# A fused layer norm, FNet and MLP kernel: the first row block multiplied before it is scaled

## The chip, the cores and the metric

The kernel runs on one core of a Trainium2 chip. A core has TensorE (PE, the matmuls; PEld is its weight load, which runs beside them), VectorE (DVE), ScalarE (ACT), GpSimd (POOL) and SyncE (SP), each with an instruction queue of its own that is worked off strictly in order. The engines wait for one another through semaphores. Data moves between DRAM and SBUF by DMA; here SP issues most of the transfers, in order. The metric is the device time of one execution in microseconds (us), median of several runs.

## The reference

The input x has 2048 rows of 640 columns. Each row is normalized, and three terms are added: x itself, a two-dimensional Fourier transform of the normalized rows (real part, as products with DFT matrices), and an MLP.

```python
def _layernorm(x, axis=-1, eps=1e-5):
    m = jnp.mean(x, axis=axis, keepdims=True)
    v = jnp.var(x, axis=axis, keepdims=True)
    return (x - m) / jnp.sqrt(v + eps)

def _A_ref(x, dft_seq_re, dft_seq_im, dft_hid_re, dft_hid_im):
    a = jnp.einsum("bsd,ed->bse", x, dft_hid_re)
    b = jnp.einsum("bsd,ed->bse", x, dft_hid_im)
    return jnp.einsum("ts,bse->bte", dft_seq_re, a) - jnp.einsum("ts,bse->bte", dft_seq_im, b)

def _B_ref(x, w1, b1, w2, b2):
    h = jnp.einsum("bsd,df->bsf", x, w1) + b1
    h = _gelu(h)
    return jnp.einsum("bsf,fd->bsd", h, w2) + b2

xn = _layernorm(x, axis=-1)
return x + _A_ref(xn, ...) + _B_ref(xn, B_w1, B_b1, B_w2, B_b2)
```

All inputs are fp32; w1 is 640 x 1536, w2 is 1536 x 640.

## The kernel before, in words

*Tiling.* The 2048 rows are four row blocks of 512; 640 columns are five chunks of 128; the 1536 hidden units are twelve groups of 128, called units here. Activations stand in SBUF transposed, columns of x on the partitions and 512 rows along the free axis, since PE contracts over partitions.

*Precision.* Every operand of a product is split in two fp32r halves: the high half is a copy made by ACT (L160), the low half is the source minus the high half, made by DVE (L161). A product is then three matmuls of 128x512: high by high, high by low, low by high (`product`, L277 to L279). One unit of the first layer for one row block, `hidden(g)` (L301), is 5 chunks times 3 = 15 matmuls into one PSUM bank (bank g % 3); one unit of the second layer, `output(g)`, is again 15 matmuls, into the five banks 3 to 7, which collect all twelve units of a row block.

*Order.* The kernel is under a manual schedule: the order of the instructions on each engine is the order in which the code issues them. No planner moves anything; semaphores alone decide when an instruction starts.

*The start.* SP loads the first four row tiles x0 to x3 (128 rows each, `load_x`, L178) and then the weights: w1 by units (`load_w1`, L255, four transfers for a unit, into three rotating buffers called w1r), w2 by units (`load_w2`). Meanwhile PE works through 19 matmuls of zeros (NWARM, L648). Their three operand tiles lie in the w1r buffers, cast from `zeros` by DVE (L639); so a load of w1 into such a buffer waits until the warm matmuls that read it are done, and NGATE says after which of them that is (the 7th, the 10th, the last). The rows are normalized one way or another: x0 by DVE statistics (`ln_stats`, L185 and L186) and a scaling on ACT, x1 by sums on ACT (L672, L676 and four one-column steps), x2 and x3 by DVE statistics and `ln_apply_chunked` (L208). `ln_scale` makes 1/sqrt(var + eps) of a variance: a square root on ACT (L192) and five small DVE steps that refine it. The normalized rows go into the tile xp, PE transposes them by chunks into banks 3 to 7 (`transpose_x`, L667), ACT and DVE split these into XTT (tile xtt, five chunks of two halves), and `hidden(0)` starts.

*The loop.* The kernel's first two row blocks make 24 steps g (twelve units each). While `output(g)` runs, `hidden(g + 2)` is already computed, and ACT's gelu (L314) turns its bank into AB, a copy (L318) makes the high half hs, a DVE subtraction (L320) the low half. The order of one step of the first row block is

```python
prep_w1(i + 3)
prep_w2(i + 1)
load_w1(i + 6)
load_w2(i + 4)
first_block(i)
acc = hidden(g + 2)
gelu(g + 2, acc)
output(g)
```

and what `first_block(i)` issues stands on DVE, ACT and SP between those:

- i = 0 and 1: the rows of the first block are scaled on DVE once more, in natural order (`ln_apply`, L201), and stored to the DRAM scratch xs (L203), from which the transposed z comes back later; the next x tiles are loaded. i = 2 to 5: statistics of x4 to x7.
- i = 6: square root, scaling and stores of these rows; the load of z for the second row block; loads of x8 to x11.
- i = 8 and 9: DVE transposes z in blocks of 32 (`transpose_z`, L238) and makes statistics of x8 to x11. In step 9, between `hidden(11)` and `gelu(11)`, the five chunks of the second block's activations are split into XTT (`prep_xt`), each behind a transpose of z.
- i = 10: `load_xo(0)`, square root, scaling and stores of x8 to x11, loads of x12 to x15.
- i = 11: the first raw columns of the hidden DFT matrices are loaded (`load_w`, tile wraw, L364), and the finished banks of the first row block are added up (`add_block`: bias on ACT L344, DVE transpose L347, add on POOL L349).

In the second row block's steps the same hands prepare the later stages: DVE turns the DFT columns (`turn_w`, L372), ACT and DVE split them into wst, POOL's queue stores them to the scratch wit (`put_w`, L394), more z is transposed and more sums are formed. Behind step 23 stand `head` and `mid`, in which ACT copies whole banks (L810, L817) so that products can go on from a copy. From 182 us on PE works through the MLP of the other row blocks and the products of the Fourier transform.

## Time and profile before

| | |
|---|---|
| median of 3 runs (lowest to highest) | 853.95 us (853.48 to 853.95) |
| profiled execution: time, span | 853.7 us, 851.9 us |
| granted TensorE clock, mean over the span | 0.998 |
| instructions | 10326 |
| busy: PE, PEld, DVE, ACT, POOL | 842.7, 695.8, 661.1, 353.6, 48.1 us |
| PE busy from 0 to 13 us | 9.74 us |
| PE busy from 13 to 182 us | 169.00 us |
| PE busy from 182 us to the end | 663.93 of 670 us |

A row of the profile's list of groups names the line of the code, the engine, the operation, the tiles written and read, the shape, how often it ran, its busy time in all and the mean of one in ns, and how long the engine idled just before them, with what ended most of that idling. A row of the timeline begins with the start in us from the start of the span and the time that the row covers (several instructions of a kind are drawn together, with their count behind the x), and ends, in square brackets, with the idle time ahead of it and the instruction that ended it. In a list of waits the three numbers are the idle time in us, how often, and the longest.

A matmul's record is longer (0.39 us) than its turn on PE (0.227 us), since successive ones overlap; the turn is what counts for the length of a stream.

### The profile page before, as it was taken

The numbers are of one execution on the slowest core, as the hardware profiler recorded it, in microseconds if no ns is written. First come the engines' busy times: TensorE is split into PE (matmuls) and PEld (weight loads), VectorE is DVE, ScalarE is ACT, GpSimd is POOL, SyncE is SP. The second block draws the span as 40 slices with busy tenths as digits, with TensorE's granted clock in tenths as the row PEclk, the third lists the DMA queues.
The fourth block names the chain that finished last, engine by engine and source line by source line (L and its number), as shares of the span: only waits on it lengthen the run. The fifth ranks groups of instructions, "written<-read, shape, count | busy, mean of one in ns | idle before, by whom it ended". The sixth has DMA issues, their size and how long they took to land.

```text
span 851.9 us, 10326 instructions
## 1 busy us (share of the span) xinstructions
PE 842.7 (99%) x3711; PEld 695.8 (82%) x3711; DVE 661.1 (78%) x836; ACT 353.6 (42%) x496; POOL 48.1 (6%) x69
## 2 busy tenths in 40 slices
PE   8999999999999999999999999999999999999997
PEld 6888888878888888888888888888888888888885
DVE  7554766785758888879979787889967998885686
ACT  7443634456666554343444343232323423222241
POOL 0000211031211300000000000000000000000001
PEclk9999999999999999999999999999999999999999
DMA  7757698937669998958744679663865779704464
GB/s 186 215 143 199 142 228 233 225 81 190 206 223 349 360 208 161 185 110 200 160 137 105 168 215 293 159 145 97 208 169 169 252 191 228 303 19 179 125 179 99
DMA packets 207235, 158.45 MB, mean 186 GB/s; under 512 B 80848, under 2 KB 180688, under 8 KB 206672
## 3 DMA queue, kind: packets, MB, share of 16 engines
q1 hardware_dynamic: 198880, 136.03, 62.6%
q0 software_dynamic: 4080, 20.97, 6.2%
q10 hardware_dynamic: 4224, 0.79, 0.4%
q8 instruction: 29, 0.48, 0.2%
q14 instruction: 22, 0.18, 0.1%
HBM read 114.76 MB, written 42.99 MB: 185 GB/s over the span
## 4 chain that ended last, share of the span: by engine, by line
PE 98%; DVE 1%; DMA 0%; ACT 0%; issue 0%; SPq 0%; ACTq 0%
PE banks L277 29%; PE banks L279 29%; PE banks L278 29%; PE banks L301 10%; DMA x<-in_A_x_dram 0%; PE banks L667 0%; DVE st L185 0%; ACT ab L672 0%; DVE yo L1695 0%; ACT mv L192 0%; DVE mv L186 0%; DVE xp L208 0%; SPq L178 0%; DVE mv L194 0%; DVE mv L196 0%
## 5 line engine op out<-in xcount | busy, mean ns | idle before, releaser
L277 PE MATMUL banks<-as,xab 128*128 128x512 f32 x411 | 159.9, 389 | 0.0
L279 PE MATMUL banks<-as,xab 128*128 128x512 f32 x411 | 159.9, 389 | 0.0
L278 PE MATMUL banks<-as,xab 128*128 128x512 f32 x411 | 159.9, 389 | 0.0
L160 ACT ACTIVATE as<-r 128x1024 fp32r<-128x1024 f32 x80 | 85.0, 1062 | 177.0 <-PE banks L279 149.2
L161 DVE TENSOR_TENSOR as<-r,as 128x1024 fp32r<-128x1024 f32 x80 | 97.2, 1216 | 41.7 <-ACT as L160 41.6
L278 PEld LDWEIGHTS banks<-as,xab 128*128 128x128 f32 x411 | 77.1, 188 | 16.1
L277 PEld LDWEIGHTS banks<-as,xab 128*128 128x128 f32 x411 | 77.1, 188 | 16.1
L279 PEld LDWEIGHTS banks<-as,xab 128*128 128x128 f32 x411 | 77.1, 188 | 16.0
L277 PE MATMUL banks<-as,xc 128*128 128x512 f32 x224 | 87.1, 389 | 0.0
L278 PE MATMUL banks<-as,xc 128*128 128x512 f32 x224 | 87.1, 389 | 0.0
L279 PE MATMUL banks<-as,xc 128*128 128x512 f32 x224 | 87.1, 389 | 0.0
L160 ACT ACTIVATE as<-rt 128x1024 fp32r<-128x1024 f32 x32 | 34.0, 1063 | 70.8 <-PE banks L279 62.8
L301 PE MATMUL banks<-xtt,xab 128*128 128x512 f32 x240 | 56.9, 390 | 0.0
L301 PEld LDWEIGHTS banks<-xtt,xab 128*128 128x128 f32 x240 | 45.0, 188 | 9.7 <-ACT xtt L160 0.5
L278 PEld LDWEIGHTS banks<-as,xc 128*128 128x128 f32 x224 | 42.0, 188 | 8.8
L279 PEld LDWEIGHTS banks<-as,xc 128*128 128x128 f32 x224 | 42.0, 188 | 8.8
L277 PEld LDWEIGHTS banks<-as,xc 128*128 128x128 f32 x224 | 42.0, 188 | 8.7
L161 DVE TENSOR_TENSOR as<-rt,as 128x1024 fp32r<-128x1024 f32 x32 | 38.8, 1212 | 5.3 <-ACT as L160 5.3
L320 DVE TENSOR_TENSOR hs<-ab,hs 128x512 fp32r<-128x512 f32 x24 | 17.6, 733 | 32.2 <-ACT hs L318 32.2
L160 ACT ACTIVATE as<-u 128x1024 fp32r<-128x1024 f32 (+1 forms) x24 | 22.1, 919 | 48.2 <-PE banks L279 48.2
L488 DVE STREAM_TRANSPOSE r<-raw 128x1024 f32<-128x1024 f32 x32 | 39.5, 1240 | 2.3 <-PE banks L279 1.8
L488 DVE STREAM_TRANSPOSE rt<-raw 128x1024 f32<-128x1024 f32 x32 | 38.8, 1230 | 0.9 <-PE banks L279 0.8
(336 smaller groups left out, 1618.2 us busy)
## 6 DMA issues: line engine op xcount, KB each, us to landing
raw<-in_A_dft_seq_re_dram SPq DMA_DIRECT2D x64, 256.0 KB, 5.8
raw<-in_A_dft_seq_im_dram SPq DMA_DIRECT2D x64, 256.0 KB, 5.1
ws<-wit SPq DMA_DIRECT2D x15, 384.0 KB, 4.1
x<-in_A_x_dram SPq DMA_DIRECT2D x16, 320.0 KB, 4.1
xs<-x SPq DMA_DIRECT2D x64, 80.0 KB, 1.8
xo<-in_A_x_dram SPq DMA_DIRECT2D x16, 320.0 KB, 6.4
xab<-wit SPq DMA_DIRECT2D x13, 384.0 KB, 4.3
wit<-wstp POOLq DMA_DIRECT2D x12, 384.0 KB, 3.9
```

The source lines that it names most:

```text
L160: nc.scalar.activation(h, s, AF.Copy)
L161: nc.vector.tensor_tensor(l, s, h.bitcast(F32), op=ALU.subtract)
L277: nc.tensor.matmul(acc, wh, mh, start=first, stop=False, skip_group_check=goes_on)
L278: nc.tensor.matmul(acc, wh, ml, start=False, stop=False, skip_group_check=goes_on)
L279: nc.tensor.matmul(acc, wl, mh, start=False, stop=last, skip_group_check=goes_on)
L301: nc.tensor.matmul(acc, W1[i][:, a, j * P : (j + 1) * P], XT[j][:, b], start=n == 0, stop=n == len(steps) - 1)
L320: nc.vector.tensor_tensor(hs[:, 1], a, hs[:, 0].bitcast(F32), op=ALU.subtract)
L488: nc.vector.transpose(held(pieces[g][2], u).rearrange("p c (n i) -> p c n i", i=B), r.rearrange("p n (c i) -> p c n i", i=B))
```

## The change

In the first row block the rows are only centred before the transposes. The products of the first layer are made from the centred rows, and each row's 1/sqrt(var + eps) is multiplied onto the result of each of the block's twelve units, on DVE, ahead of the gelu. The factor is a number per row, and rows lie along the free axis there, so it has to stand on all 128 partitions: ACT writes each factor 128 times side by side (`wide`), four PE transposes inside `hidden(2)` (`spread`, after its first ASIDE = 4 matmuls) turn that into bank 7, and DVE copies it to the tile RB, which takes one of the two places with the tag yt.

With it go these edits. x0 and x2 get their means from the DVE statistics and x1 and x3 from sums on ACT; the variances of x1 and x3 are made later, by ACT's squares of the centred rows behind `hidden(1)`'s operands, and one square root for all four tiles follows there; a gelu of one column comes ahead of the spreading copy. The warm matmuls are 12 instead of 19, with one operand tile that lies in the place "as" and no longer in w1's buffers, so that w1's first three loads wait for none of them; the load of w1's first unit is cut in two (chunks 0 and 1, then 2 to 4), and its halves are split in two parts as well. w1's third unit is split between the squares and the square root, ahead of the split of w2's first unit instead of behind it. `output(0)` runs its 15 matmuls in another order: for all five banks those with the high half of hs first, then those with the low half.

```diff
--- before.py
+++ after.py
@@ -17,9 +17,9 @@
 Q = 4
 B = 32
 EPS = 1e-5
-NWARM = 19
-NGATE = (7, 10)
+NWARM = 12
 TAIL = 4
+ASIDE = 4
 PADL = 8
 
 
@@ -245,14 +245,15 @@
 
     W1, W2, w1r, w2r = {}, {}, {}, {}
 
-    def load_w1(i, eng=nc.sync):
+    def load_w1(i, eng=nc.sync, cuts=(0, ND)):
         if i >= NF:
             return
         t = early.tile([P, ND, P], F32, tag="w1r", bufs=3, name=f"w1r{i}")
         w1r[i] = t
...
-        for q in range(Q):
-            eng.dma_start(t[q * B : (q + 1) * B], v[q, :, :, i * P : (i + 1) * P])
+        for c0, c1 in zip(cuts, cuts[1:]):
+            for q in range(Q):
+                eng.dma_start(t[q * B : (q + 1) * B, c0:c1], v[q, :, c0:c1, i * P : (i + 1) * P])
 
     def load_w2(i, eng=nc.sync):
         if i >= NF:
@@ -286,7 +287,7 @@
     def unit(g):
         return g if g < NF else LATE[g % NF]
 
-    def hidden(g):
+    def hidden(g, aside=None):
         i = unit(g)
         acc = bank(g % 3)
         kinds = ((0, 0), (0, 1), (1, 0))
@@ -297,6 +298,8 @@
 
             steps.sort(key=lambda s: s[1] == 2)
         for n, (j, k) in enumerate(steps):
+            if aside and n == ASIDE:
+                aside()
             a, b = kinds[k]
             nc.tensor.matmul(
                 acc, W1[i][:, a, j * P : (j + 1) * P], XT[j][:, b], start=n == 0, stop=n == len(steps) - 1
@@ -311,6 +314,9 @@
 
         i = unit(g)
         a = AB[:, g % 2]
+        if g < NF:
+            nc.vector.tensor_tensor(a, acc, RB, op=ALU.mult)
+            acc = a
         nc.scalar.activation(a, acc, AF.Gelu_apprx_tanh, bias=b1c[:, i : i + 1])
         fill(0)
         hs = HS[:, g % 3]
@@ -319,11 +325,27 @@
         fill(1)
         nc.vector.tensor_tensor(hs[:, 1], a, hs[:, 0].bitcast(F32), op=ALU.subtract)
 
+    def first_output(hs):
+        w = W2[0]
+        for k in range(2):
+            for e in range(ND):
+                cols = slice(e * P, (e + 1) * P)
+                if k == 0:
+                    nc.tensor.matmul(oacc[0][e], w[:, 0, cols], hs[:, 0], start=True, stop=False)
+                    nc.tensor.matmul(oacc[0][e], w[:, 1, cols], hs[:, 0], start=False, stop=False)
+                else:
+                    nc.tensor.matmul(
+                        oacc[0][e], w[:, 0, cols], hs[:, 1], start=False, stop=False, skip_group_check=True
+                    )
+
     def output(g):
         t, i = divmod(g, NF)
         if i == 0:
             oacc[t] = [bank(3 + e) for e in range(ND)]
-        second(t, i, unit(g), HT[g])
+        if g == 0:
+            first_output(HT[g])
+        else:
+            second(t, i, unit(g), HT[g])
 
     def second(t, i, u, hs, es=range(ND)):
         for e in es:
@@ -628,23 +650,26 @@
 
     zeros = rows.tile([P, TB], F32, tag="yt", bufs=2, name="zeros")
 
-    warms = [early.tile([P, TB], F32R, tag="w1r", bufs=3, name=f"warm{k}") for k in range(3)]
+    RB = rows.tile([P, TB], F32, tag="yt", bufs=2, name="rb")
 
     for c in range(NC):
         load_x(c)
+    for tag, size, keys in PLACES:
+        t = whole[tag] = place(tag, (P, size // 4))
+        for k, key in enumerate(keys):
+            slots[key] = t[:, k * 2 * D : (k + 1) * 2 * D].rearrange("p (a b) -> p a b", a=2)
     nc.gpsimd.memset(eps, EPS)
     make_identity(nc, ident)
     nc.vector.memset(zeros, 0.0)
-    for warm in warms:
-        nc.vector.tensor_copy(warm, zeros)
+    warm = whole["as"][:, :TB]
+    nc.vector.tensor_copy(warm, zeros)
 
     nc.scalar.activation(eps[:, 1:2], eps[:, 0:1], AF.Sqrt)
-    load_w1(0)
+    load_w1(0, cuts=(0, 2, ND))
     load_w1(1)
 
     wacc = bank(0)
     for k in range(NWARM):
-        warm = warms[sum(k >= n for n in NGATE)]
         nc.tensor.matmul(wacc, warm[:, :P], warm, start=True, stop=True)
     load_w1(2)
     load_w2(0)
@@ -652,10 +677,6 @@
     load_w2(1)
     load_w2(2)
 
...
     for j in range(ND):
         new_xt(0, j)
     tacc = [bank(3 + j) for j in range(ND)]
@@ -667,50 +688,55 @@
             nc.tensor.transpose(tacc[j][:, c * P : (c + 1) * P], xp[:, c, j * P : (j + 1) * P], ident)
 
 
-    m = MV[:, 1]
-    scratch = AB.rearrange("p a b -> p (a b)")
-    nc.scalar.activation(scratch[:, :D], xt[1], AF.Copy, accum_out=m[:, 4:5])
-    ln_stats(0)
-    ln_scale(0, 1)
-    nc.scalar.activation(m[:, 5:6], m[:, 4:5], AF.Copy, scale=-1.0 / D)
-    nc.scalar.activation(scratch[:, :D], xt[1], AF.Square, bias=m[:, 5:6], accum_out=m[:, 2:3])
-    nc.scalar.activation(m[:, 1:2], m[:, 2:3], AF.Copy, scale=1.0 / D)
-    nc.scalar.activation(m[:, 0:1], m[:, 5:6], AF.Copy, scale=-1.0)
-
-    def center(c):
-        n = MV[:, c]
-        nc.vector.scalar_tensor_tensor(n[:, 5:6], n[:, 0:1], -1.0, n[:, 3:4], op0=ALU.mult, op1=ALU.mult)
-
-    def apply_on_act(c, j0, j1):
-        n = MV[:, c]
-        nc.scalar.activation(
+    scratch = AB.rearrange("p a b -> p (a b)")[:, :D]
+
+    def sum_on_act(c):
+        nc.scalar.activation(scratch, xt[c], AF.Copy, scale=-1.0 / D, accum_out=MV[:, c, 5:6])
+
+    def square_on_act(c):
+        nc.scalar.activation(scratch, xp[:, c], AF.Square, scale=D**-0.5, accum_out=MV[:, c, 1:2])
+
+    def center(c, op, shift, j0=0, j1=ND):
+        nc.vector.tensor_scalar(
             chunked(xp[:, c])[:, :, j0:j1],
             xt[c].rearrange("p (q c i) -> p q c i", q=Q, i=B)[:, :, j0:j1],
-            AF.Identity,
-            bias=n[:, 5:6],
-            scale=n[:, 3:4],
+            shift,
+            None,
+            op0=op,
         )
 
-    center(0)
-    apply_on_act(0, 0, ND)
-    for c in (2, 3):
-        ln_stats(c)
+    W1[0], first_w1 = slots[1, 0], w1r.pop(0).rearrange("p a b -> p (a b)")
+
+    def first_hi(j0, j1):
+        nc.scalar.activation(W1[0][:, 0, j0 * P : j1 * P], first_w1[:, j0 * P : j1 * P], AF.Copy)
+
+    def first_lo(j0, j1):
+        h, l = (W1[0][:, k, j0 * P : j1 * P] for k in range(2))
+        nc.vector.tensor_tensor(l, first_w1[:, j0 * P : j1 * P], h.bitcast(F32), op=ALU.subtract)
+
+    sum_on_act(1)
+    nc.scalar.activation(
+        chunked(xp[:, 1]), xt[1].rearrange("p (q c i) -> p q c i", q=Q, i=B), AF.Identity, bias=MV[:, 1, 5:6]
+    )
+    ln_stats(0)
+    center(0, ALU.subtract, MV[:, 0, 0:1])
+    ln_stats(2)
+    center(2, ALU.subtract, MV[:, 2, 0:1])
+    sum_on_act(3)
+    center(3, ALU.add, MV[:, 3, 5:6], 0, 2)
+    center(3, ALU.add, MV[:, 3, 5:6], 2, ND)
+    first_hi(0, 2)
+    first_lo(0, 2)
     transpose_x(0, 0, ND)
-    ln_scale(1, 3)
-    center(1)
-
-    W1[0], first_w1 = slots[1, 0], w1r.pop(0).rearrange("p a b -> p (a b)")
+    transpose_x(1, 0, ND)
     for j0, j1 in ((0, 2), (2, ND)):
-        apply_on_act(1, j0, j1)
-        if j0 == 0:
-            nc.scalar.activation(W1[0][:, 0], first_w1, AF.Copy)
-        for c in (2, 3, 1):
-            if c != 1:
-                ln_apply_chunked(xp[:, c], c, j0, j1)
-            transpose_x(c, j0, j1)
-    nc.vector.tensor_tensor(W1[0][:, 1], first_w1, W1[0][:, 0].bitcast(F32), op=ALU.subtract)
+        transpose_x(2, j0, j1)
+        transpose_x(3, j0, j1)
     for j in range(ND):
         split(XT[j][:, 0], XT[j][:, 1], tacc[j])
+        if j == 1:
+            first_hi(2, ND)
+            first_lo(2, ND)
     load_w1(3)
     load_w1(4)
     for q in range(Q):
@@ -718,8 +744,28 @@
     acc0 = hidden(0)
     prep_w1(1)
     acc1 = hidden(1)
+
+    nc.gpsimd.tensor_scalar(MV[:, 1::2, 0], MV[:, 1::2, 5], -1.0, None, op0=ALU.mult)
+    square_on_act(1)
+    square_on_act(3)
+    W1[2] = slots[1, 2]
+    raw2 = w1r.pop(2).rearrange("p a b -> p (a b)")
+    nc.scalar.activation(W1[2][:, 0], raw2, AF.Copy)
+    ln_scale(0, NC)
+    nc.scalar.activation(eps[:, 1:2], eps[:, 0:1], AF.Gelu_apprx_tanh)
+    nc.vector.tensor_tensor(W1[2][:, 1], raw2, W1[2][:, 0].bitcast(F32), op=ALU.subtract)
+    wide = AB[:, 1]
+    nc.scalar.activation(
+        wide.rearrange("p (c n) -> p c n", c=NC), MV[:, :, 3:4].broadcast_to([P, NC, P]), AF.Copy
+    )
+
+    def spread():
+        for c in range(NC):
+            nc.tensor.transpose(bank(7)[:, c * P : (c + 1) * P], wide[:, c * P : (c + 1) * P], ident)
+
+    acc2 = hidden(2, spread)
     prep_w2(0)
-    prep_w1(2)
+    nc.vector.tensor_copy(RB, bank(7))
     load_w2(3)
     load_w1(5)
 
@@ -1023,7 +1069,7 @@
                 output(g)
                 gelu(g + 2, hidden(g + 2))
             else:
-                acc = hidden(g + 2)
+                acc = hidden(g + 2) if g else acc2
                 if i == NF - 3:
                     for j in range(ND):
                         prep_xt(1, j)
```

More of the change, by code (lines that the diff above doesn't have):

```diff
@@ L653 @@
     load_w2(2)
-    for tag, size, keys in PLACES:
-        t = whole[tag] = place(tag, (P, size // 4))
-        for k, key in enumerate(keys):
-            slots[key] = t[:, k * 2 * D : (k + 1) * 2 * D].rearrange("p (a b) -> p a b", a=2)
     for j in range(ND):
```

## The prediction

> **What bounds the kernel now.** I read the page first (engines, chain), then what PE waited for, then the first 30 us and the stretch from 57 to 182 us as a timeline.
>
> ```profile
> span 851.9 us, 10326 instructions
> ...
> PE 842.7 (99%) x3711; PEld 695.8 (82%) x3711; DVE 661.1 (78%) x836; ACT 353.6 (42%) x496; POOL 48.1 (6%) x69
> ...
> PE 98%; DVE 1%; DMA 0%; ACT 0%; issue 0%; SPq 0%; ACTq 0%
> ```
>
> PE is busy 99% of the span and carries 98% of the chain, so the time is the moment at which PE's stream begins plus every gap in it. Only two lists of waits matter: PE's own at the start, and its weight loads' (PEld), which show where ACT or DVE already arrive at the last moment.
>
> ```profile
> PE banks L667 <- DVE xp L208: 1.3, 1, 1.3
> ```
>
> ```profile
> PEld banks L277 <- ACT banks L810: 0.5, 2, 0.3
> ```
>
> The first is the layer norm ahead of the transposes. The second lies at 182 us: there ACT has no room at all, and whatever is late on ACT or DVE by then is paid by PE. The median of the runs is 853.95; the profiled execution took 853.7 (851.9 and 1.8 around the span), 0.25 less, and I add the change to the median.
>
> **Part 1: the start.** Rows of the first 30 us, and two groups and a landing view of the same stretch:
>
> ```profile
> 3.77 0.89 DVE L185 BATCH_NORM_STATS2 st<-x 128x6 f32<-128x320 f32 x2 [1.23 <-DMA x<-in_A_x_dram]
> ...
> 9.85 1.51 DVE L208 TENSOR_SCALAR xp<-x,mv 128x256 f32<-128x256 f32 x4
> ...
> 21.12 0.69 DVE L320 TENSOR_TENSOR hs<-ab,hs 128x512 fp32r<-128x512 f32 x1 [1.63 <-ACT hs L318]
> 21.75 0.82 DVE L161 TENSOR_TENSOR xab<-w1r,xab 128x640 fp32r<-128x640 f32 x1
> ```
>
> ```profile
> 4.51 0.74 ACT L672 ACTIVATE ab<-x 128x640 f32<-128x640 f32 x1 [2.28 <-DMA x<-in_A_x_dram]
> ...
> 5.65 0.83 ACT L676 ACTIVATE ab<-x,mv 128x640 f32<-128x640 f32 x1
> ...
> 11.70 2.52 ACT L160 ACTIVATE xtt<-banks 128x512 fp32r<-128x512 f32 x5
> ...
> 16.12 1.28 ACT L314 ACT_TABLE_LOAD   x1
> 17.41 0.69 ACT L314 ACTIVATE ab<-banks,b1c 128x512 f32<-128x512 f32 x1
> 18.13 0.63 ACT L318 ACTIVATE hs<-ab 128x512 fp32r<-128x512 f32 x1
> ```
>
> ```profile
> 6.68 0.62 PE L648 MATMUL banks<-warm 128*128 128x512 f32 x2
> ```
>
> ```profile
> 8.27 0.71 PE L667 MATMUL banks<-ident,xp 128*128 128x128 f32 x5
> ...
> 12.33 10.76 PE L301 MATMUL banks<-xtt,xab 128*128 128x512 f32 x45
> ...
> 26.33 3.56 PE L301 MATMUL banks<-xtt,xab 128*128 128x512 f32 x15
> ```
>
> ```profile
> L639 DVE CAST warm<-zeros 128x512 fp32r<-128x512 f32 x3 | 1.1, 422 | 0.0
> ```
>
> ```profile
> L161 DVE TENSOR_TENSOR xtt<-banks,xtt 128x512 fp32r<-128x512 f32 x5 | 3.1, 683 | 0.2 <-ACT xtt L160 0.2
> ```
>
> ```profile
> L178 SPq DMA_DIRECT2D x<-in_A_x_dram x4: 407/420/432, 0.7 to 2.1; - x4
> ...
> DMA to landing us min/median/max: 3.0/3.6/4.3
> ```
>
> *Centering.* Square roots leave the path to the transposes. The twelfth warm product ends its turn at 6.68 (the thirteenth starts there), so PE is free then, not at 8.27. x0: statistics at 3.77, 1.1 with their aggregate, one centering of 640 columns at about 0.6 (1.51 for 1280, and a start): 5.5. x1: sum on ACT 4.51 and 0.9, shift 0.9: 6.3. x2 lands at about 5.6: 7.4. x3 lands at 2.1 + 4.3 = 6.4, sum 0.9, first piece 0.4: 7.75. Twenty transposes, 0.11 apart (five in 0.71, one 0.27), run from 6.68: PE's turn for x3 comes at 8.0, after its data. ACT copies the first chunk from 8.3, hidden(0) starts at 8.93 instead of 12.33.
>
> *hidden(0) to hidden(2).* The halves of w1's first unit now stand between the chunk copies (0.44 more on ACT, 0.5 on DVE), which puts 0.8 of gaps into hidden(0): it ends at 13.05 (fifteen turns of 0.227, hidden(3)'s 3.4 in the rows, and the 0.8). hidden(1) ends at 16.45.
>
> *The scale's own chain.* ACT: last chunk 11.2, w1(1) 0.63, two squares 0.95 each, w1(2) 0.63: square root at 14.2. The root and the five small DVE steps behind it take 1.16 (94.48 to 95.64, quoted below): 15.36. Table 1.28, a dummy gelu 0.2, the spreading copy 0.63: 16.5. PE reaches the four transposes after four products of hidden(2), at 17.36, so that chain has 0.9 of room; the transposes lengthen PE by 0.44. Their bank is read from 18.0 (w2's first low half ends there on DVE too). The copy to RB from PSUM shows nowhere: between 0.42 (a cast in SBUF) and 0.68 (a two-operand read of PSUM); I take 0.6, nearer the PSUM row. Multiply 0.69, gelu 0.72, high half 0.63: 20.75. PE finished hidden(2) at 20.3 and waits 0.5. output(0) has the same 15 products in another order: nothing. Behind it DVE does low half, next multiply, then ACT gelu and copy, then DVE low half and w1(3): 4.24 more, so hidden(3)'s third product starts at 25.03 against 26.33 + 0.45 = 26.78. That is 1.75; gelu reads SBUF instead of PSUM, some 0.04 twice: PE leads by **1.7**.
>
> *Edits that cost nothing here.* Seven warm products, two casts and four one-column ACT steps go; POOL gets one tiny step, with nothing behind it until 100 us. w1's first loads are issued from 2.6 instead of 5.3 with four more issues on SP; SP then waits for landings and reaches w2 when it did before. What the ungated loads may cost is rival C. Range of the lead: 0.9 to 2.1.
>
> **Part 2: twelve new multiplies on DVE.** Each stands between hidden(g) and its gelu, so gelu and all that ACT and DVE queue behind it start 0.73 later against PE. Mostly that is covered: ACT waits 4.19 for PE per unit (57.13 below). It isn't where ACT and DVE feed something else. Rows:
>
> ```profile
> 57.13 0.69 ACT L314 ACTIVATE ab<-banks,b1c 128x512 f32<-128x512 f32 x1 [4.19 <-PE banks L301]
> ...
> 91.21 0.67 ACT L314 ACTIVATE ab<-banks,b1c 128x512 f32<-128x512 f32 x1
> ...
> 94.48 0.30 ACT L192 ACTIVATE mv<-mv,eps 128x4 f32<-128x4 f32 x1
> ```
>
> ```profile
> 62.87 7.33 SPq L203 DMA_DIRECT2D xs<-x  x16
> ...
> 96.29 7.31 SPq L203 DMA_DIRECT2D xs<-x  x16
> ...
> 105.58 5.34 SPq L364 DMA_DIRECT2D wraw<-in_A_dft_hid_re_dram  x4
> ```
>
> ```profile
> 79.96 0.71 DVE L238 STREAM_TRANSPOSE zt<-z 128x512 f32<-128x512 f32 x1 [5.65 <-DMA z<-xs]
> ...
> 82.62 0.65 DVE L320 TENSOR_TENSOR hs<-ab,hs 128x512 fp32r<-128x512 f32 x1
> 83.18 0.82 DVE L161 TENSOR_TENSOR r<-w2r,r 128x640 fp32r<-128x640 f32 x1
> ...
> 91.33 0.69 DVE L161 TENSOR_TENSOR xtt<-zt,xtt 128x512 fp32r<-128x512 f32 x1 [0.19 <-ACT xtt L160]
> ...
> 95.64 2.18 DVE L201 TENSOR_SCALAR x<-x,mv 128x640 f32<-128x640 f32 x4
> ```
>
> ```profile
> 90.93 6.96 PE L301 MATMUL banks<-xtt,xab 128*128 128x512 f32 x30
> ```
>
> ```profile
> 112.86 0.85 DVE L372 STREAM_TRANSPOSE wt<-wraw 128x640 f32<-128x640 f32 x1 [3.37 <-DMA wraw<-in_A_dft_hid_re_dram]
> ```
>
> ```profile
> 131.83 0.42 ACT L160 ACTIVATE wst<-wt 128x256 fp32r<-128x256 f32 x1 [1.69 <-DMA wit<-wst]
> ...
> 154.43 0.42 ACT L160 ACTIVATE wst<-wt 128x256 fp32r<-128x256 f32 x1 [2.93 <-DMA wit<-wst]
> ...
> 175.45 0.60 ACT L817 ACTIVATE fifth<-banks 128x512 f32<-128x512 f32 x1 [0.78 <-PE banks L279]
> ...
> 181.49 0.58 ACT L810 ACTIVATE banks<-banks 128x512 f32<-128x512 f32 x1 [2.39 <-DVE ab L347]
> ```
>
> All times here are those of before; against PE's own clock (which runs 1.7 early) the steps slip so:
> 1. gelu(7) is 0.73 late, and with it the square root after it, the stores to xs (62.87) and z's landing: DVE's transpose at 79.96 slips 0.73.
> 2. DVE's order puts multiply(10) behind that transpose and two statistics, where before only a low half stood whose gelu was long done. Now DVE multiplies (0.69), idles for gelu and copy (0.72 and 0.67), and only then makes the low half: 82.62 becomes 85.47, w2's low half 86.10 instead of 83.18, 2.92 late. The five chunks of the second block's activations follow on DVE without a gap (83.18 to 91.33), the last ends at 94.94 instead of 92.02. hidden(12) reads it in its fourteenth product, at 90.93 + 13 times 0.227 = 93.88: PE waits 1.1.
> 3. gelu(11), before at 91.21 ahead of the last low half, must now follow multiply(11) behind it: 94.25 + 0.63 + 0.69 + 0.04 = 95.61, **4.4** late, and so are the square root (94.48), the scaling (95.64) and the stores (96.29).
> 4. SP issues from 96.29 without a gap to the loads of the hidden DFT matrices (105.58); DVE waits 3.37 for them (112.86), ACT waits for stores of what it made of them (131.83, 154.43, and others between), and from 156 to 181 DVE works almost without a gap up to the transpose that ACT's copy at 181.49 waits for. No wait of this run is one for PE but that of 175.45, whose removal gives back 0.43. PE has no room there: it gets 4.4 - 0.4 = 4.0 late, the 1.1 of step 2 being inside it.
>
> Sum: -1.7 + 4.0 = **+2.3**, 853.95 + 2.3 = 856.25. From then on PE, ACT and DVE are late alike. Bounds of the 4.0: 3.4 if the many short hand-overs of step 4 leave 0.6 of slack that I can't see, 4.2 if the copy at 175.45 gives back only half. With the lead's range: 855.3 to 857.2.
>
> The spreading needs a table change beside hidden(1). The row says 1.28 at 16.12 and a gelu at 17.41 right behind, no more. The Trainium skill ("ScalarE: Activation LUTs", section "What ACT_TABLE_LOAD costs") adds a drain of about 1380 ns to each switch. By that the copy would end at 17.9, past PE's 17.36, the lead would be 1.2 and the time 856.7 (rival D).
>
> **Rivals.**
> A. *Transfers absorb step 4.* DVE's 3.37 at 112.86 and ACT's 1.69 and 2.93 are waits for DMA; if those landings are set by traffic and not by when they were issued, the delay dies there and PE pays only hidden(12): -1.7 + 1.1, 853.4. For it: the waits are long. Against: the loads come from the same SP queue that is late.
> B. *PE keeps its lead (faster).* If the second block's chunks slip less than the 1.86 that hidden(12) leaves (93.88 - 92.02), step 2 costs nothing, and with A's absorption the time is 853.95 - 1.7 = 852.25. It takes a z that lands over 1.06 sooner. Against: DVE waited 5.65 for z, so z is late, not early.
> C. *Ungated w1 loads slow x2 and x3.* The four x, 320 KB each, land from 3.7 (0.7 + 3.0) to 6.4, one in 0.9 us; the first cut's 128 KB is 0.35 at that rate, 0.7 if its shorter rows go at half of it. That moves PE's start one for one beyond 0.25 of room: 856.7; with the second cut in front too, 857.4.
> D. The table's drain, above: 856.7. That fewer warm products leave PE's clock low I give nothing: 4 us without products (8.27 to 12.33) didn't lower it.
>
> **How the numbers follow.** Forecast 0.55, A 0.20, B 0.12, C 0.10, D and others 0.03. 0.2% (1.7 us) is about what can be told from no change: below 852.24 half of B and a little of A, 0.09; above 855.66 nine tenths of the forecast, C and D, 0.60; between them 0.31. The likeliest is 856.2, its own range 855.3 to 857.2; to hold 8 in 10 the range reaches over A, 853.0, and to C, 857.6.
>
> **What would show it.** Right: hidden(0) at 8.9, hidden(3)'s third product near 25.0; DVE's low half of unit 10 waiting about 1.4 for ACT behind a multiply that follows z's transpose; a PE gap of about 1 near 92; stores to xs from about 99; a gap of about 2 at 182 behind ACT's copy. Wrong: no gap at 182 (A), or hidden(0) past 9.7 (C). The forecast fails most simply if step 3's delay doesn't reach the wraw loads.

## The result and the profile after

The changed kernel takes 857.25 us (median of 6 runs, 856.39 to 857.56) against 853.96 of the kernel before in the same comparison (853.48 to 854.48): ratio 1.0035, 95% interval 1.0025 to 1.0044, so 3.3 us slower with 2.1 to 3.8 possible. The forecast was 856.2, range 853.0 to 857.6.

The changed kernel's page, its first two rows, and then the list of what its PE waited for (total, times, longest):

```profile
span 854.8 us, 10321 instructions
...
PE 844.0 (99%) x3708; PEld 695.0 (81%) x3708; DVE 667.2 (78%) x838; ACT 354.1 (41%) x497; POOL 49.0 (6%) x70
```

```profile
PE banks L673 <- DVE as L665: 1.9, 1, 1.9
PE banks L278 <- ACT banks L856: 0.8, 1, 0.8
PE banks L304 <- DVE xtt L161: 0.7, 2, 0.4
PE banks L334 <- ACT hs L324: 0.4, 1, 0.4
PE banks L688 <- DVE xp L700: 0.4, 1, 0.4
PE banks L278 <- DVE ot L369: 0.3, 1, 0.3
```

Before, PE waited only for the warm operands and for the layer norm. Now it also waits for the first hs (L334), for DVE's chunks of the second block (L304), for the turned banks of the first block (ot) and for ACT's bank copy (L856). The profiled execution took 856.57, 0.7 less than the median; its span is 2.9 longer than that of before.

How far the streams stand apart can be read from one unit of the first layer at three places. PE's rows for hidden(4), hidden(14) and hidden(23) in the timeline of the kernel before, then of the changed one:

```profile
33.13 3.56 PE L301 MATMUL banks<-xtt,xab 128*128 128x512 f32 x15
101.13 3.56 PE L301 MATMUL banks<-xtt,xab 128*128 128x512 f32 x15
162.33 3.56 PE L301 MATMUL banks<-xtt,xab 128*128 128x512 f32 x15
```

```profile
32.72 3.56 PE L304 MATMUL banks<-xtt,xab 128*128 128x512 f32 x15
102.33 3.56 PE L304 MATMUL banks<-xtt,xab 128*128 128x512 f32 x15
164.11 3.56 PE L304 MATMUL banks<-xtt,xab 128*128 128x512 f32 x15
```

PE leads by 0.41 at hidden(4), is late by 1.20 at hidden(14) (so 1.61 were lost in hidden(12)), by 1.78 at hidden(23) (0.58 in output(12), behind the transposes ot), and by 2.9 at the end: 0.9 come at 182 to 185 us, the last 0.2 behind that. Net, a lead of 0.4 and, between the two profiled executions, a loss of 3.3; by the medians the loss is 3.7.

*The start*, rows of the changed kernel's timeline on ACT, DVE and PE:

```profile
7.56 0.74 ACT L694 ACTIVATE ab<-x 128x640 f32<-128x640 f32 x1 [1.39 <-DMA x<-in_A_x_dram]
...
15.23 1.28 ACT L755 ACT_TABLE_LOAD   x1
16.52 0.20 ACT L755 ACTIVATE eps<-eps 128x1 f32<-128x1 f32 x1
```

```profile
6.81 0.89 DVE L185 BATCH_NORM_STATS2 st<-x 128x6 f32<-128x320 f32 x2 [1.39 <-DMA x<-in_A_x_dram]
...
15.24 0.18 DVE L194 RECIPROCAL mv<-mv 128x4 f32<-128x4 f32 x1 [0.65 <-ACT mv L192]
...
19.06 0.69 DVE L768 COPY rb<-banks 128x512 f32<-128x512 f32 x1 [0.33 <-PE banks L764]
...
25.36 0.83 DVE L161 TENSOR_TENSOR xab<-w1r,xab 128x640 fp32r<-128x640 f32 x1
```

```profile
6.97 1.25 PE L688 MATMUL banks<-ident,xp 128*128 128x128 f32 x10
8.59 1.37 PE L688 MATMUL banks<-ident,xp 128*128 128x128 f32 x10 [0.36 <-DVE xp L700]
9.88 8.71 PE L304 MATMUL banks<-xtt,xab 128*128 128x512 f32 x34
```

ACT idles for x3 until 7.56 (the forecast had it at 6.4), DVE for x2 until 6.81. The transposes start at 6.97, behind the twelfth warm product, and not at 6.68; after ten of them PE stands for x2; hidden(0) starts at 9.88, not at 8.93. w1(3)'s low half, which hidden(3)'s third product waits for, ends at 26.2, not at 25.0.

*The second block's hand-overs*, rows of the same timeline on DVE, ACT, SP, PE's weight loads and PE:

```profile
80.72 0.71 DVE L238 STREAM_TRANSPOSE zt<-z 128x512 f32<-128x512 f32 x1 [6.06 <-DMA z<-xs]
...
83.35 0.64 DVE L318 TENSOR_TENSOR ab<-banks,rb 128x512 f32<-128x512 f32 x1
85.44 0.69 DVE L326 TENSOR_TENSOR hs<-ab,hs 128x512 fp32r<-128x512 f32 x1 [1.46 <-ACT hs L324]
...
94.22 0.69 DVE L161 TENSOR_TENSOR xtt<-zt,xtt 128x512 fp32r<-128x512 f32 x1 [0.18 <-ACT xtt L160]
...
116.84 0.85 DVE L394 STREAM_TRANSPOSE wt<-wraw 128x640 f32<-128x640 f32 x1 [2.80 <-DMA wraw<-in_A_dft_hid_re_dram]
```

```profile
95.55 0.72 ACT L320 ACTIVATE ab<-ab,b1c 128x512 f32<-128x512 f32 x1 [1.36 <-DVE ab L318]
...
184.15 0.58 ACT L856 ACTIVATE banks<-banks 128x512 f32<-128x512 f32 x1 [2.64 <-DVE ab L369]
```

```profile
100.68 7.33 SPq L203 DMA_DIRECT2D xs<-x  x16
```

```profile
92.77 0.53 PEld L304 LDWEIGHTS banks<-xtt,xab 128*128 128x128 f32 x3 [0.79 <-DVE xtt L161]
94.09 0.53 PEld L304 LDWEIGHTS banks<-xtt,xab 128*128 128x128 f32 x3 [0.79 <-DVE xtt L161]
```

```profile
184.78 0.50 PE L278 MATMUL banks<-xtt,tw 128*128 128x512 f32 x1 [0.79 <-ACT banks L856]
```

The same product in the kernel before:

```profile
182.13 0.50 PE L277 MATMUL banks<-xtt,tw 128*128 128x512 f32 x1
```

DVE multiplies unit 10 behind z's transpose and the statistics (83.35), idles 1.46 for gelu and copy, and makes the low half at 85.44 where it stood at 82.62 before: 2.8 late. The last chunk is 2.9 late (94.22 against 91.33); twice PE's weight load waits 0.79 for such a chunk. gelu(11) is 4.3 late (95.55 against 91.21), the stores to xs 4.4 (100.68 against 96.29), DVE's first transpose of wraw 4.0 (116.84 against 112.86), ACT's bank copy only 2.7 (184.15 against 181.49), and so is the product behind it (184.78 against 182.13).

### The profile page after: what moved, and what is told of

It is laid out like the page before. It is cut to its first block, busy times and chain, and to the rows that moved or that the text cites. A ratio compares the mean times of both kernels' runs of the same rounds, so it can differ in the third digit from the quotient of the medians.

```text
span 854.8 us, 10321 instructions
## 1 busy us (share of the span) xinstructions
PE 844.0 (99%) x3708; PEld 695.0 (81%) x3708; DVE 667.2 (78%) x838; ACT 354.1 (41%) x497; POOL 49.0 (6%) x70
## 4 chain that ended last, share of the span: by engine, by line
PE 81%; DMA 6%; DVE 4%; SPq 3%; issue 2%; ACT 2%; POOL 0%; DVEq 0%; ACTq 0%; POOLq 0%
PE banks L278 26%; PE banks L279 26%; PE banks L280 26%; PE banks L304 2%; DMA wit<-wst 2%; DMA rq<-in_B_w_dram 1%; DMA z<-xs 1%; SPq L386 1%; SPq L203 1%; DMA x<-in_A_x_dram 1%; SPq L256 1%; DMA w2r<-in_B_w_dram 1%; DVE xtt L161 0%; DVE x L201 0%; DVE zt L238 0%
## 5 line engine op out<-in xcount | busy, mean ns | idle before, releaser
L304 PE MATMUL banks<-xtt,xab 128*128 128x512 f32 x240 | 58.9, 395 | 0.8 <-DVE xtt L161 0.7
L304 PEld LDWEIGHTS banks<-xtt,xab 128*128 128x128 f32 x240 | 44.4, 188 | 12.6 <-DVE xtt L161 2.2
L161 DVE TENSOR_TENSOR as<-u,as 128x1024 fp32r<-128x1024 f32 (+1 forms) x24 | 24.9, 1042 | 18.8 <-ACT as L160 18.8
```

What stands on the lines that cost most here:

```text
L161: nc.vector.tensor_tensor(l, s, h.bitcast(F32), op=ALU.subtract)
L304: nc.tensor.matmul(acc, W1[i][:, a, j * P : (j + 1) * P], XT[j][:, b], start=n == 0, stop=n == len(steps) - 1)
```

## The experiments

The theory, from the prediction: two of the twelve multiplies, those of units 10 and 11, carry nearly all of the loss, by where they stand on DVE; and PE's lead shrank since w1's ungated loads delay x2 and x3. The rivals: the loss is the added work of all twelve; the lead is set by something else. Where a comparison gives a ratio, it is to the kernel before in the same comparison.

### The two late multiplies, left out; the early ones, left out

```diff
-        if g < NF:
+        if g < NF - 2:
             nc.vector.tensor_tensor(a, acc, RB, op=ALU.mult)
```

> Leaves out the multiplies of units 10 and 11 of the first row block (their gelu reads the bank unscaled); the other ten stay. Theory (these two, by their place on DVE behind z's transpose and ahead of gelu(11), carry nearly all of the cost): no gap of PE in hidden(12), DVE's last chunk of the second block ends near 92.8, stores to xs begin near 97.3 instead of 100.7, and the time is 853.6 to 854.3. Rival (the cost is spread over the twelve, 0.3 each): 857.25 less two twelfths of 3.7, 856.6.

853.50 us, ratio 0.9995 (0.9986 to 1.0004). The theory holds; the rival asked for 856.6. Its stores to xs begin at 97.26, where the theory had them.

```diff
-        if g < NF:
+        if g in (0, 1, NF - 2, NF - 1):
             nc.vector.tensor_tensor(a, acc, RB, op=ALU.mult)
```

> Leaves out the multiplies of units 2 to 9; those of units 0, 1, 10 and 11 stay. Theory (two late multiplies carry the cost, multiply(7) only moves z by its own 0.7): z's transpose at 80.0 instead of 80.7, the gaps of PE in hidden(12) and at 182 us each shrink by up to 0.7 and stay otherwise, time 856.5 to 857.2. Rival (spread over the twelve): eight twelfths of 3.7 go, 854.8.

856.29 us, ratio 1.0029 (1.0020 to 1.0038), just below the theory's 856.5 to 857.2 and far from the rival's 854.8; its profiled execution has z's transpose at 79.57. Of the two gaps only one shrank: PE waits 0.2 instead of 0.7 in hidden(12), but 1.6 instead of 0.8 for the bank copy at 182 us. Without eight of the twelve most of the loss is left, without the other two all of it is gone. How the loss divides between these two no run shows; they were left out and moved together.

### The same work at other places

```diff
+    def scaled(g, acc):
+        a = AB[:, g % 2]
+        nc.vector.tensor_tensor(a, acc, RB, op=ALU.mult)
+        return a
...
-            first_block(i)
+            if i != NF - 4:
+                first_block(i)
...
                 if i == NF - 3:
+                    acc = scaled(g + 2, acc)
                     for j in range(ND):
                         prep_xt(1, j)
...
                 gelu(g + 2, acc)
+                if i == NF - 4:
+                    first_block(i)
```

`gelu` itself then multiplies for g up to 10 only. Step 8 so makes unit 10 before z is transposed, and unit 11 is multiplied ahead of the five chunks.

> The changed kernel with two places exchanged on DVE and nothing left out: step 8 makes multiply(10), gelu(10) and its low half before z's first transpose and the statistics of x8 and x9, and multiply(11) stands ahead of the five chunks of the second block instead of behind them. Theory (place, not work): multiply(10) runs near 77.2, the last chunk ends near 92.8, before PE needs it at 93.5, gelu(11) follows at once near 92, the stores begin near 97.2; the gap in hidden(12) goes and that at 182 us shrinks to nothing or 0.5, time 853.5 to 854.3. Rival (the added work itself costs, wherever it stands): 856.5 to 857.3.

853.38 us, ratio 0.9995 (0.9986 to 1.0004). Rows of its timeline (multiply(10), then multiply(11), the last chunk; then gelu(11) on ACT), and all that its PE waits for behind the warm products:

```profile
76.89 0.69 DVE L315 TENSOR_TENSOR ab<-banks,rb 128x512 f32<-128x512 f32 x1 [2.46 <-PE banks L304]
...
86.37 0.64 DVE L315 TENSOR_TENSOR ab<-banks,rb 128x512 f32<-128x512 f32 x1
...
91.75 0.69 DVE L161 TENSOR_TENSOR xtt<-zt,xtt 128x512 fp32r<-128x512 f32 x1 [0.18 <-ACT xtt L160]
```

```profile
91.62 0.71 ACT L324 ACTIVATE ab<-ab,b1c 128x512 f32<-128x512 f32 x1
```

```profile
PE banks L338 <- ACT hs L328: 0.4, 1, 0.4
PE banks L692 <- DVE xp L704: 0.4, 1, 0.4
PE banks L278 <- ACT banks L860: 0.2, 1, 0.2
```

multiply(10) now falls into time in which DVE only waited for z; the last chunk is 0.4 late instead of 2.9, gelu(11) 0.4 instead of 4.3, and of the waits behind 30 us only 0.2 at 182 are left. All twelve multiplies are still there. So the loss is the place, not the work.

### The multiplies alone, in the kernel before

```diff
+    RB = rows.tile([P, TB], F32, tag="yt", bufs=2, name="rb")
...
+    nc.gpsimd.memset(RB, 1.0)
...
         a = AB[:, g % 2]
+        if g < NF:
+            nc.vector.tensor_tensor(a, acc, RB, op=ALU.mult)
+            acc = a
```

> The kernel before with the second part of the change alone: a tile of ones is multiplied onto the twelve units of the first row block, ahead of their gelu, at the same places on DVE. Theory (the cost is the multiplies' places, the new start gains 0.4): 853.84 + 3.3 + 0.4 = 857.5. Rival (part of the loss comes from the new start): 856.5 or less.

858.68 us (855.63 to 860.23), ratio 1.0052 (1.0039 to 1.0065), so 3.3 to 5.5 us of loss; the theory's 857.5 lies inside, 1.2 below the median. In its profiled execution PE waits 0.6 for the chunks (L301) and 1.5 for ACT's bank copy (L815). The rival is out: no part of the loss needs the new start. The same kernel with the two multiplies ahead, by the edit above:

> The kernel before with the twelve multiplies by ones, of which that of unit 10 (with its gelu and low half) now stands ahead of z's first transpose and that of unit 11 ahead of the second block's five chunks. Theory (two places carry the cost): 854.0 to 854.8. Rival (the work of twelve multiplies costs wherever it stands): 857 or more.

853.88 us, ratio 1.0001 (0.9993 to 1.0010). With the old start as with the new one, twelve multiplies at good places cost nothing that can be measured.

### The wait at 182 us

```diff
         form_of("s3", 1, two(4)[:, 1], XTT[:, 2])
+
+    def after_s3():
+        outs(1, (0,), yt=lambda n: AB[:, 0], done=False)
         add(two(2), two(2), ZT, ALU.subtract)
...
             output(g)
+            after_s3()
...
-    outs(1, (0,), yt=lambda n: AB[:, 0], done=False)
```

> The changed kernel with one step moved: the bias and transpose of the second block's first finished bank, for which ACT's bank copy and then PE wait at 182 to 185 us, stand on ACT and DVE right behind the forms s3, ahead of one sum, one split of 1024 columns and one of 512 (2.8 us of DVE). Theory (PE pays at 182 only because this chain ends last there): the gap at 184.8 goes, PE's delay stays what it is ahead of it (-0.4 + 1.6 + 0.6 = 1.8), time 855.7. Rival (DVE as a whole is late by then, and the next form takes the place of the wait): 856.8 or more.

856.30 us, ratio 1.0026 (1.0015 to 1.0037): between the two. A wait of the profiled execution, 857.33 and the slowest of the seven, says why:

```profile
PE banks L278 <- DVE zs L369: 1.3, 1, 1.3
```

The wait for ACT's bank copy is gone and PE waits for the next banks that DVE turns (zs). As the rival had it, DVE as a whole is late there; moving one step of it hands the wait on. How much of the 0.9 by which the median fell is the move itself, the runs don't settle.

### The start: which transfers delay x

```diff
+NGATE = (7, 10)
...
+    warms = [early.tile([P, TB], F32R, tag="w1r", bufs=3, name=f"warm{k}") for k in range(3)]
...
-    warm = whole["as"][:, :TB]
-    nc.vector.tensor_copy(warm, zeros)
+    for warm in warms:
+        nc.vector.tensor_copy(warm, zeros)
...
     for k in range(NWARM):
+        warm = warms[sum(k >= n for n in NGATE)]
```

> The changed kernel with one thing undone: the twelve warm products read three tiles that lie in w1's buffers, so that w1's first three loads wait for the 7th, the 10th and the last of them, as before the change. Theory (w1's ungated loads crowd x2 and x3): x3's sum starts near 6.4 instead of 7.56, hidden(0) starts near 9.0 instead of 9.88, PE's lead at hidden(4) over the kernel before grows from 0.41 to about 1.3, and since the late hand-overs of the second block are tied to PE's own clock, the time falls by about 0.9 to 856.3. Rival (x2 and x3 are late for another reason, or the scale's chain alone sets the lead): hidden(0) stays at 9.8 to 9.9 or the lead stays at 0.4, and the time stays at 857.2.

856.59 us, ratio 1.0035 (1.0024 to 1.0046): no gain that can be told. Its timeline on ACT (x3's sum, then the two halves of w1's first unit) and PE:

```profile
6.51 0.74 ACT L697 ACTIVATE ab<-x 128x640 f32<-128x640 f32 x1 [0.18 <-DMA x<-in_A_x_dram]
...
8.50 0.42 ACT L714 ACTIVATE xab<-w1r 128x256 fp32r<-128x256 f32 x1 [1.16 <-DMA w1r<-in_B_w_dram]
...
10.39 0.53 ACT L714 ACTIVATE xab<-w1r 128x384 fp32r<-128x384 f32 x1 [0.49 <-DMA w1r<-in_B_w_dram]
```

```profile
9.46 1.45 PE L305 MATMUL banks<-xtt,xab 128*128 128x512 f32 x4 [0.58 <-ACT xtt L161]
11.45 7.11 PE L305 MATMUL banks<-xtt,xab 128*128 128x512 f32 x30 [0.54 <-ACT xtt L161]
```

Gated, x3 is there by 6.51 instead of 7.56. But ACT now idles for both cuts of w1: hidden(0) starts behind a wait at 9.46, not at 9.0, waits 0.54 more after four products, and the lead at hidden(4) is 0.43, as the rival had it.

One execution of each kernel doesn't show, though, that the gate is what brought x3 sooner. The start of the changed kernel stands unchanged in four of the runs above, so the record has five executions of it; rows of the one without the eight early multiplies, on ACT (x3's sum) and PE (the twenty transposes, then hidden(0) and what follows):

```profile
6.38 0.74 ACT L694 ACTIVATE ab<-x 128x640 f32<-128x640 f32 x1
```

```profile
7.19 2.65 PE L688 MATMUL banks<-ident,xp 128*128 128x128 f32 x20
9.77 8.67 PE L304 MATMUL banks<-xtt,xab 128*128 128x512 f32 x34
```

| ungated start, profiled execution of | slowest of the four x, issue to landing | x3's sum | first transpose | hidden(0) | lead at hidden(4) |
|---|---|---|---|---|---|
| the changed kernel | 5.4 | 7.56 | 6.97 | 9.88 | 0.41 |
| without the two late multiplies | 5.8 | 7.92 | 6.78 | 10.21 | 0.10 |
| without the eight early ones | 4.2 | 6.38 | 7.19 | 9.77 | 0.55 |
| with multiplies 10 and 11 ahead | 5.2 | 7.37 | 6.80 | 9.66 | 0.65 |
| with the bank turned earlier | 4.6 | 6.73 | 7.19 | 9.72 | 0.61 |

The four executions in which w1 waits for the warm products (the kernel before, its two versions with ones, the gated one) have 4.3, 4.4, 5.2 and 4.4 in the second column. The two ranges overlap, so that w1's free loads delay x is not shown. Nor does hidden(0) follow x3 alone: with x3 there at 6.38 PE goes through its transposes without a wait, and starts hidden(0) at 9.77 all the same, because its twelfth warm product is done only at 7.19 and the transposes take 2.6.

The next run was to show which part of w1's load does the harm:

```diff
         for c0, c1 in zip(cuts, cuts[1:]):
+            if c0:
+                nc.sync.dma_start(b1c, b1.rearrange("(i p) -> p i", p=P))
+                for q in range(Q):
+                    s = b2[q * DQ : (q + 1) * DQ].rearrange("(c i) -> i c", i=B)
+                    nc.sync.dma_start(b2c[q * B : (q + 1) * B], s)
             for q in range(Q):
...
-    nc.sync.dma_start(b1c, b1.rearrange("(i p) -> p i", p=P))
...
-    for q in range(Q):
-        nc.sync.dma_start(b2c[q * B : (q + 1) * B], b2[q * DQ : (q + 1) * DQ].rearrange("(c i) -> i c", i=B))
```

> The changed kernel with one order of SP changed: the five tiny loads of the biases (2.3 us of SP's issuing) stand between the two cuts of w1's first unit instead of behind. Theory (x2 and x3 share the DMA engines with w1's first unit, and only its first cut is needed early): x3's sum starts near 6.9 to 7.0 instead of 7.56, hidden(0) near 9.3 instead of 9.88, the lead at hidden(4) near 0.9 instead of 0.41, time 856.7. Rival (what x gains, the second cut of w1 loses, as when the loads were gated): hidden(0) or its later products wait for w1, the lead stays 0.4 and the time 857.2.

858.98 us, ratio 1.0058 (1.0046 to 1.0070): worse than either had it. Its SP and ACT rows:

```profile
4.95 3.51 SPq L259 DMA_DIRECT2D b2c<-in_B_b_dram  x4
```

```profile
7.59 0.74 ACT L698 ACTIVATE ab<-x 128x640 f32<-128x640 f32 x1 [1.25 <-DMA x<-in_A_x_dram]
...
11.84 0.52 ACT L715 ACTIVATE xab<-w1r 128x384 fp32r<-128x384 f32 x1 [1.52 <-DMA w1r<-in_B_w_dram]
```

x3 is as late as in the changed kernel (7.59) although the second cut is issued only at 8.5. That doesn't clear the second cut: the bias loads were in flight in its place (of the packets under 512 bytes in the first 7 us this kernel has 1209, the changed one 151), and by the table 7.59 is no unusual value. What the run does show is the price of the order: the four loads of b2, 0.6 KB each, held SP for 3.51 us, not the 1.9 that they took at 19 us in the changed kernel, so the second cut came 1.5 too late for ACT.

### Versions with all moves

The first took the multiplies ahead, the bank turned earlier, the bias loads between the cuts, and at the start these edits (the multiplies of units 0 and 1 ahead of the low half of w2's first unit, the spreading after one product):

```diff
-ASIDE = 4
+ASIDE = 1
...
+    nc.vector.tensor_copy(RB, bank(7))
+    acc0, acc1 = scaled(0, acc0), scaled(1, acc1)
     prep_w2(0)
-    nc.vector.tensor_copy(RB, bank(7))
```

> A version that should beat both: the two multiplies ahead as in the fourth run, the bank turned earlier as in the run before this one, SP's five tiny bias loads between the two cuts of w1's first unit, and at the start the spreading transposes after one product of hidden(2) instead of four, with the multiplies of units 0 and 1 ahead of the low half of w2's first unit on DVE. Expected by theory: hidden(0) starts near 9.3, no wait at output(0), hidden(3) without the wait for w1's low half, PE's lead 1.7 to 1.9 at hidden(4) and kept to the end, time 852.2. Rival (a lead over the kernel before can't be kept, since DVE's and ACT's chain is bound by transfers): a wait of PE near 92 or 182 takes it back, 853.4.

855.19 us, ratio 1.0013 (1.0004 to 1.0021), more than either had forecast. The bias loads spoiled its start (hidden(0) at 10.53, then 1.74 of waiting for w1), yet behind the start PE waited for nothing more. Without them:

> The version with all moves, less the one that failed: the bias loads stand behind w1's again. Theory: hidden(0) near 9.8 as in the changed kernel, no wait at output(0) and none of hidden(3) for w1's low half, PE's lead at hidden(4) 1.2 instead of 0.4, nothing of it given back, time 852.6 (0.9985 of the kernel before). Rival (a lead can't be kept past 92 and 182 us): a wait of PE there and 853.4 or more.

852.69 us, ratio 0.9984 (0.9976 to 0.9993): faster than both, as forecast. All waits of its PE behind the warm products, hidden(4), and the bank copy at 179 us, which now waits for PE and not for DVE:

```profile
PE banks L692 <- DVE xp L704: 1.1, 1, 1.1
```

```profile
31.86 3.56 PE L304 MATMUL banks<-xtt,xab 128*128 128x512 f32 x15
```

```profile
178.94 0.58 ACT L861 ACTIVATE banks<-banks 128x512 f32<-128x512 f32 x1 [1.08 <-PE banks L280]
```

The lead of 33.13 - 31.86 = 1.27 is kept to the end (span 850.5, 1.4 less than before). It doesn't come from x: hidden(0) starts at 10.11, later than in the changed kernel, but the waits for the first hs and for w1(3)'s low half are gone. Two more versions of the start on top of this one, first the loads of x2 and x3 issued from ACT's queue, then the edit of the gated kernel with its gate set earlier (shown against that edit):

```diff
-        load_x(c)
+        load_x(c, nc.scalar if c > 1 else nc.sync)
```

> The tenth run's kernel with the loads of x2 and x3 issued by ACT's queue beside x0 and x1 from SP's, so that all four are issued by about 1.6 and w1's first unit by SP from about 1.7. Theory (x2 and x3 are late because w1's first cut shares the DMA engines with them): w1's cut starts earlier too and the order of landing hardly changes, x3's sum 7.0 to 7.6, lead 1.2 to 1.7, time 852.1 to 852.6. Rival (issuing is the limit): x3's sum before 6.6, hidden(0) before 9.0, time 851.7.

852.45 us, ratio 0.9981 (0.9972 to 0.9989). On ACT:

```profile
0.73 0.91 ACTq L178 DMA_DIRECT2D x<-in_A_x_dram  x2
...
6.32 0.74 ACT L698 ACTIVATE ab<-x 128x640 f32<-128x640 f32 x1 [3.15 <-DMA x<-in_A_x_dram]
```

Issued side by side, x1 is there for its sum at 6.32 instead of 4.69; x3's sum follows on ACT at 7.92 without a wait, and hidden(0) starts at 10.19, no earlier than 10.11. What the sooner issue saves, x1 loses. The Trainium skill ("DMA: Bandwidth & Descriptors", section "Issuing engines are not separate DMA queues") says that DMAs of different engines run on the same 16 DMA engines and interleave; this run agrees, with x1 1.6 later.

```diff
-NGATE = (7, 10)
+NGATE = (4, 8)
```

> The tenth run's kernel with w1's first loads gated again, but earlier than before the change: behind the 4th and the 8th of the twelve warm products instead of the 7th and the 10th. Theory (with no gate x3 lands 1.1 late; with the old gate w1's cuts land 1.1 late): issued from about 3.8, the first cut lands by 7.8 and delays x3 by half, x3's sum near 7.0, the second cut lands before 10, hidden(0) near 9.3, lead 1.6 to 1.8, time 852.1. Rival (bytes, not order, set it): hidden(0) at 9.5 or later, as both ends gave, lead 1.2, time 852.6.

852.38 us, ratio 0.9981 (0.9972 to 0.9990); x3's sum at 7.36, hidden(0) at 9.65, hidden(4) at 31.37, a lead of 1.76, of which PE gives some back in a wait of 0.3 for ACT's bank copy. The lead is the theory's, hidden(0)'s start the rival's, at the low end of the table above; of the last three versions the times can't be told apart, and what a still better order of x and w1 would give stays open.

## Why the prediction was right, and where its steps were off

The direction, and the mechanism of the loss, were right; the time lay in the range, 1.0 above the forecast value and at the upper end of the forecast's own 855.3 to 857.2. But both terms of the sum were too large. The lead came out 1.3 smaller, the loss 0.3 to 0.7, and as they have opposite signs the sum is nearer than its larger error: that part is luck.

1. *The lead, predicted 1.7, measured 0.41* (0.10 to 0.65 in the five executions with this start). hidden(0) starts 0.95 later than forecast, and two readings taken from one trace are behind most of it. "The twelfth warm product ends its turn at 6.68": here it is 6.97, 0.29 later. "x3 lands at 2.1 + 4.3 = 6.4": here x2 and x3 are late, and PE stands 0.53 between the tenth transpose (its turn ends at 8.06) and the eleventh (8.59). The remaining 0.13 lie in the transposes themselves, which take 2.38 without that wait, not 2.25. Neither reading is a constant of this start: the first transpose stands at 6.78 to 7.19 in the five, x3's sum at 6.38 to 7.92. Behind hidden(0) another 0.3 goes: gaps in the three units of 1.0 instead of 0.8, the copy to RB, and so w1(3)'s low half 1.2 later; PE's wait for hs is 0.39 instead of 0.5.
2. *Step 1, z 0.73 late against PE's clock.* Measured 0.76 in absolute time, 1.17 against a PE that leads by 0.41: stores and loads of z lost the other 0.4 on their way.
3. *Step 2, the chunks 2.92 late, PE waits 1.1.* The chunks are 2.89 late in absolute time, 3.30 against PE; the difference to 2.92 is z's 0.4. PE lost 1.61.
4. *Step 3, gelu(11) 4.4 late behind multiply(11).* 4.34 in absolute time, 4.75 against PE: again z's 0.4 more.
5. *Step 4, 4.0 by 182 us.* Between the profiled executions it is 3.1 by 185 us and 3.3 in all, below the bounds of 3.4 to 4.2; by the medians, 3.3 slower and a lead of 0.4, it is 3.7 and within them. Of the 4.4 at SP's stores, 0.4 are gone at the first transpose of wraw (DVE's wait for it shrank from 3.37 to 2.80) and another 1.3 by ACT's bank copy, of which 0.43 had been foreseen. So rival A's absorption at wraw is real, but a tenth of the 4.4.
6. *Edits costed at nothing*: the RB copy took 0.69 instead of the estimated 0.6; no trace of the fewer warm products in the clock (0.999 over the span). SP reaches w2 at 11.73 instead of 10.96, and nothing in the list of waits comes of it.

Three sums of the prediction don't come out as written: its hidden(0) ends at 13.13 and not at 13.05, its square root stands at 14.36 and not at 14.2, its x3 is ready at 7.70 and not at 7.75. None of them moves the forecast by more than 0.1.

Rival B (the lead kept, 852.25) fell by both its conditions; with the two multiplies moved, the bank turned earlier and the start reordered a lead was kept (852.69). Rival C's sign came, since hidden(0) starts past 9.7, and the lost lead is larger than the 0.45 that it cost in the forecast; but its cause, w1's loads, isn't shown by the runs, and its 857.4 is not worked out from anything. Rival D fell: the gelu of one column starts at 16.52, behind a table load that ends at 16.51, and the square root ahead of the load had handed its result to DVE by 15.24. So the drain of the Trainium skill's "ScalarE: Activation LUTs" ("What ACT_TABLE_LOAD costs") isn't seen in this run.

## What to carry to other kernels

An added instruction on an engine with idle time costs what stands behind it in that engine's order: ask of each copy of it which wait it is put behind and who waits for the next instruction, as two of these twelve cost nearly all and ten next to nothing. A landing or a start that is read from one trace is one draw: five executions of one start had the slowest load of x at 4.2 to 5.8 us and a lead of 0.10 to 0.65, so give such a term a range, and look at several traces before another load is blamed. And a late step on a chain that ends last elsewhere is seldom cured where the wait shows: moving one step at 182 us gave the wait to the next, moving the cause at 80 us left 0.2 of it.

## What was not expected of the hardware

- The slowest of four loads of 320 KB took 4.2 to 5.8 us from issue to landing in five executions of one and the same start, though the issues stood at 0.73 to 2.13 each time.
- The twelve warm products end their last turn at 6.78 to 7.19 in these five. In the two with 7.19 the twelve took 0.44 each from 1.90 on, against the 0.227 of later products; in the kernel before, 1.92 to 6.68, 0.40 each. At what moment the pace rises differs from execution to execution, and no run shows what sets it.
- Four loads of 0.6 KB each, with single elements scattered, held SP for 3.51 us right behind another scattered load, of which the first alone took 2.07; at 19 us four took 1.88.
- Some kernels vary more from run to run: 855.63 to 860.23 with the ones at their first place, 853.62 to 854.73 with two of them moved. That each landing of z and wraw reaches PE directly where the chain of DVE and ACT ends last would explain it, but no run isolates it, and the changed kernel with the two multiplies moved still ranges over 852.46 to 855.09.
